# Attention and MLP-mixer kernel: raw buffers of its own for one of the last four weight rows, and v of a unit loaded by one transfer

## The chip, the cores and the metric

The kernel runs on one core of one Trainium2 chip. Five engines work side by side on a core: TensorE (PE, with its weight loads shown apart as PEld), VectorE (DVE), ScalarE (ACT), GpSimd (POOL) and SyncE (SP), which here only issues transfers. The metric is the device time of one execution in microseconds; smaller is better. Several executions are timed, and their median is the kernel's time. One further execution is recorded by the hardware profiler, and all rows shown are from such a record.

## The reference

A linear attention (softmax of q over its features, softmax of k over the sequence) gives a row block x of 576 tokens by 512 features for each of 8 batches, and a mixer follows: one small MLP over the tokens, one over the channels. The weights w come as 64-bit floats, everything else as 32-bit floats.

```python
q_s = softmax(q, axis=-1); k_s = softmax(k, axis=2)        # 8 x 8 heads x 576 x 64
kv = np.einsum('bhsd,bhse->bhde', k_s, v)
x = np.einsum('bhsd,bhde->bhse', q_s, kv)                  # as 8 x 576 x 512
h = np.maximum(xt @ w_tok1, 0.0) @ w_tok2                  # xt: x with tokens last, 576 -> 256 -> 576
u = x + h.transpose(0, 2, 1)
h2 = np.maximum(u @ w_ch1, 0.0) @ w_ch2                    # 512 -> 1536 -> 512
return (u + h2).astype(np.float32)
```

## The kernel before

**Units and groups.** The attention and the token MLP go by units: one batch and two heads, 128 columns, 32 units in all (NU). The channel MLP goes by groups of 512 tokens, nine in all (NG). The first eight units (two batches, NE) are worked off first, in an early stage with buffers of its own; from then on the remaining units are woven into the channel MLP of earlier groups.

**The channel MLP.** w_ch1 and w_ch2 are cut into twelve rows f of 128 hidden features (NF). A step of the list `steps` is one group and one row: `ch1` multiplies the group's u by row f of w_ch1 into a PSUM bank (L482), ACT and DVE turn that into a high part and a low part of h (L485, L486), and one step later `ch2` multiplies h by row f of w_ch2 into four accumulators (L642). The list runs group 0 with rows 0 to 3, group 1 with rows 0 to 11, group 0 with rows 4 to 11 (24 steps up to n0), and then the other groups. From group 3 on the products are made pairwise by a faster scheme (`pair_a`, `pair_b`, L593) out of matrices that were prepared from the rows and written to memory.

**Loading a weight row.** Each weight is a 64-bit number, and the kernel makes 32-bit ones of them itself. `load_weights` brings a piece of 128 x 512 raw numbers (512 KB) into a raw tile by SP (L196). `narrow` does the conversion: DVE takes the exponent out (L232), ACT rescales it (L233), DVE puts in the sign (L234), makes the fraction (L235, L237) and multiplies the two (L239) into a tile cv_s. Then `split` writes a high part by ACT (L130) and a low part by DVE (L131) into the row's place in c1h and c1l, or c2h and c2l. The narrowed piece of w_ch1 is also stored to memory from cv_s by ACT's queue (`whole`, L290). Rows 0 to 7 go two at a time through wide raw tiles (`load_pair`, L222); rows 8 to 11 one at a time (`load_ch`), at steps 7, 8, 10 and 11, each with two pieces: one of w_ch1 and one of w_ch2. Raw tiles come from the pool stg, which has two buffers of 4 KB per partition; cv_s has two buffers too, and `stage_qT` of a unit uses one of them for its transposed q (L393), from which DVE and ACT copy 32-wide blocks (L403) before q's high part qth is cast (L130) for `stage_u` (L459).

**Room.** Pools are stacks on two sides of the on-chip memory. When the early stage ends, its room goes to the tiles of the later units, to c2 of rows 4 to 7, and to the wide raw tiles stg_x and cv_x of rows 4 to 7 (24 KB per partition). When rows 8 to 11 begin, stg_x and cv_x close, and in their place come c2 (16 KB) and c1 (16 KB) of rows 8 to 11. A tile that lies where another lay waits for that one's last reader. After group 2's last steps `stage_pair_pools` closes the c1 pools and puts the pair scheme's tiles there.

**Loading a unit.** `load_unit` brings k transposed (kt), q and k by one transfer each, `load_v` brings v: two transfers of 128 partitions x 4 blocks x 64 (one for each head, L184) and one for the last 64 tokens (L185). In v's tile each block of 64 has a 65th column of ones, so that one matmul (L355) gives both kv and the sum of k; rows 64 to 127 of the last block are zeros, written once by POOL. From unit 8 on there is one v tile, and v of the next unit is asked for when the matmuls on this one are issued.

**What sets the order.** The program is written in one order, and a planner lays out each engine's own order from it when the program is built, with a simulated timeline (`schedule_with_timeline_sim=True`); at run time each engine and each queue goes in that order, so that an instruction whose input is late holds up those behind it. SP's queue takes all loads of weights, q, k and v. `behind(drained)` holds the narrowing of a row, on ACT and DVE, behind the h of the step before.

Of the kernel before, what the change touches and what calls it, by code (L numbers as in the profile page):

```python
# [15 lines left out]
P = 128  # L16
# [4 lines left out]
def attn_mixer_kernel(ctx: ExitStack, tc: tile.TileContext, q, k, kt, v, wt, out, dims):  # L21
# [3 lines left out]
    nc = tc.nc  # L25
    B, H, S, D, TOK, DM, DCH, wide = dims
    NJ = DM // P
    NF = DCH // P
    NT = TOK // P
    C = S // P  # L30
    C1 = C + 1
    S0 = C * P
    TL = S - S0
    NG = B * S // CW
    NU = B * NJ
    NE = 2 * NJ
    F_HEAD, F_MORE = 4, 8
    G_S = 3
    WIDE1, WIDE2 = False, False
    EP = (2, 4)  # L40
# [7 lines left out]
    stg = ctx.enter_context(tc.tile_pool(name="stg", bufs=2))  # L48
    cv = ctx.enter_context(tc.tile_pool(name="cv", bufs=2))
# [10 lines left out]
    def v_tile(pool):  # L60
        t = pool.tile([P, C1, 2, D + 1], F32, name="v_t")
        nc.gpsimd.memset(t[:, :, :, D : D + 1], 1.0)
        nc.gpsimd.memset(t[TL:P, C, :, :], 0.0)
        return t

    v_ring = [v_tile(const)]

    ones = const.tile([P, P], F32, name="ones")
# [24 lines left out]
    c1, c1_pools = {}, {}  # L93

    def c1_rows(f0, f1, side):
        c1_pools[f0] = ExitStack()
        pool = c1_pools[f0].enter_context(tc.tile_pool(name=f"c1_{f0}", bufs=1, side=side))
        t = [pool.tile([P, f1 - f0, NJ, P], F32R, name=f"c1{x}{f0}") for x in "hl"]
        for f in range(f0, f1):
            c1[f] = t, f - f0  # L100
# [8 lines left out]
    def c2_rows(f0, f1):  # L109
        late = ctx.enter_context(tc.tile_pool(name=f"late{f0}", bufs=1))  # L110
        h_ = late.tile([P, f1 - f0, DM], F32R, name=f"c2h{f0}")
        l_ = late.tile([P, f1 - f0, DM], F32R, name=f"c2l{f0}")
        for f in range(f0, f1):
            c2[f] = (h_, l_), f - f0
# [30 lines left out]
    conv = [(stg, cv)]  # L145
    first = []

    @contextmanager
    def behind(instructions):
        with ExitStack() as stack:  # L150
            for ins in instructions:
                stack.enter_context(tc.issue_after(ins))
            yield
# [26 lines left out]
    def load_v(n):  # L180
        if n < NU and n not in v_of:
            t = v_ring[n % 2 if n < NE else 0]
            for h in range(2):
                nc.sync.dma_start(t[:, 0:C, h, 0:D], v[n][:, 0:C, h * D : (h + 1) * D])  # L184
            nc.sync.dma_start(t[0:TL, C, :, 0:D], v[n][0:TL, C, :].rearrange("p (h d) -> p h d", h=2))  # L185
            v_of[n] = t

    def load_weights(i, n=CW, out=None):
# [285 lines left out]
    def ch1(g, f):  # L474
        hh, hl = (h2[:, x, f % 2, :] for x in range(2))
        t = ps_h.tile([P, 512], F32, name="ps_h")
        wh, wl = c1_row(f)
        i = 0
        for n in range(NJ):
            uh, ul = (x[:, n, :] for x in uT[g])  # L480
            for a, w in ((wh, uh), (wl, uh), (wh, ul)):
                nc.tensor.matmul(t, a[:, n, :], w, start=(i == 0), stop=(i == 3 * NJ - 1))  # L482
                i += 1
        drained[:] = [
            nc.scalar.activation(hh, t, AF.Relu).ins,  # L485
            nc.vector.scalar_tensor_tensor(hl, t, 0.0, f32(hh), op0=ALU.max, op1=ALU.subtract).ins,  # L486
        ]
        return hh, hl
# [33 lines left out]
    ring, T, tf, odd, h_slots = [], [], [], [], []  # L522

    def stage_pair_pools(f0):
        c1_pools[f0].close()
        if f0 == 0:
            pool = ctx.enter_context(tc.tile_pool(name="pairs_a", bufs=1, side="right", reuse_waits="tile"))
            for x in "hl":
                T.append(pool.tile([P, 4, CW], F32R, name=f"t{x}"))
            tf.extend(pool.tile([P, CW], F32, name=f"tf{i}") for i in range(2))  # L530
            ring.extend(pool.tile([P, 4, P], F32R, name=f"ring{i}") for i in range(6))
        else:
            pool = ctx.enter_context(tc.tile_pool(name="pairs_b", bufs=1, reuse_waits="tile"))
            odd.extend(pool.tile([P, 2 * CW], F32, name=f"c{i}") for i in range(2))
            h_slots.extend((h2[:, 0, i], h2[:, 1, i]) for i in range(2))
            h_slots.append(tuple(pool.tile([P, CW], F32R, name=f"h3{x}") for x in "hl"))
            ring.extend(pool.tile([P, 4, P], F32R, name=f"ring{i}") for i in range(6, 8))
# [11 lines left out]
    rows = {}  # L549
# [49 lines left out]
    def pair_a(g, p):  # L599

        x = ps_h.tile([P, 512], F32, name="ps_h")
        product(g, P1, x, A)
        product(g, P6, x, Bq)
        c = odd[p % 2]
        c11, both, c22 = c[:, 0:HW], c[:, HW : 3 * HW], c[:, 3 * HW :]
        nc.scalar.copy(c11, x[:, A])
        nc.vector.tensor_tensor(c22, x[:, Bq], c11, op=ALU.add)
        y = ps_h.tile([P, 512], F32, name="ps_h")
        product(g, P5, y, A)
        product(g, P7, y, Bq)  # L610
        nc.vector.tensor_tensor(halves(both), halves(y[:, 0:CW]), c22.unsqueeze(1).broadcast_to([P, 2, HW]), op=ALU.add)
        nc.vector.tensor_tensor(c22, y[:, A], both[:, Bq], op=ALU.add)
        held[0] = c, c11, both

    def pair_b(g, p):

        c, c11, both = held.pop(0)
        x = ps_h.tile([P, 512], F32, name="ps_h")
        product(g, P2, x, A)
        nc.vector.tensor_tensor(c11, x[:, A], c11, op=ALU.add)  # L620
        z = ps_h.tile([P, 512], F32, name="ps_h")
        product(g, P3, z, A)
        product(g, P4, z, Bq)
        nc.vector.tensor_tensor(both, z, both, op=ALU.add)  # L624
        out = []
        for r in (slice(0, CW), slice(CW, 2 * CW)):
            hh, hl = h_slots[at_h[0] % 3]
            at_h[0] += 1
            nc.scalar.activation(hh, c[:, r], AF.Relu)  # L629
            nc.vector.scalar_tensor_tensor(hl, c[:, r], 0.0, f32(hh), op0=ALU.max, op1=ALU.subtract)  # L630
            out.append((hh, hl))
        return out

    def ch2(acc, f, first, last, hh, hl, in_turn=False):

        at = []
        wh, wl = c2_row(f)
        for n, o in enumerate(acc):
            cs = slice(n * P, (n + 1) * P)
            for i, (a, w) in enumerate(((wh, hh), (wl, hh), (wh, hl))):  # L640
                with behind(at):
                    m = nc.tensor.matmul(o, a[:, cs], w, start=(first and i == 0), stop=(last and i == 2))  # L642
                if in_turn:
                    at = [m.ins]
# [79 lines left out]
    load_tok1()  # L724
    first = []
    load_v(0)
    begin(1)
    stages[0][0]()
    soft(1)
    stages[0][1]()  # L730
    load_v(1)
    load_tok2()
    conv[:] = [(stg, cv)]
# [19 lines left out]
    c2_rows(F_HEAD, F_MORE)  # L753
    more_pools = ExitStack()
    wide_pools[:] = [more_pools.enter_context(tc.tile_pool(name=n, bufs=2)) for n in ("stg_x", "cv_x")]

    unit_banks[0] = (ph,)

# [32 lines left out]
    for g in range(2, NG):  # L791
# [8 lines left out]
        put(at - 2, lambda g=g: data_sums(g, (0, 1, 2)))  # L800
        put(at - 1, lambda g=g: data_sums(g, (3,)))
    put(n0 + 8, lambda: stage_pair_pools(0))
    put(n0 + 9, lambda: [load_product() for _ in range(6)])
    put(n0 + 11, lambda: stage_pair_pools(F_MORE))
    put(n0 + 11, lambda: [load_product() for _ in range(2)])

    pend = []
    acc_of = {}
    load_at = {1: F_HEAD, 4: F_HEAD + 2, **dict(zip((7, 8, 10, 11), range(F_MORE, NF)))}
    for i, (g, f) in enumerate(steps):  # L810
        if i in load_at:
            if load_at[i] == F_MORE:
                more_pools.close()
                c2_rows(F_MORE, NF)
                c1_rows(F_MORE, NF, None)
            with behind(drained):
                (load_ch if load_at[i] >= F_MORE else load_pair)(load_at[i])
        more = []
        if g < G_S:
            more = [(f, ch1(g, f))]  # L820
        elif f % 2 == 0:
            pair_a(g, f // 2)
        else:
            more = list(zip((f - 1, f), pair_b(g, f // 2)))
        for fn in todo.pop(i, []):
            fn()
        if pend:
            now = pend.pop(0)
            ch2(*now[1:])
            if now[4]:  # L830
                out_end(*now[:2], i != F_HEAD)
        for fn in todo.pop(i + 0.5, []):
            fn()
        last = i + 1 == len(steps) or steps[i + 1][0] != g
        for ff, h in more:
            new = i == 0 or (g < G_S and steps[i - 1][0] != g) or (g >= G_S and ff == 0)
            if new:
                acc = [ps_o.tile([P, CW], F32, name="ps_o") for _ in range(NJ)]
            pend.append((g, acc, ff, new, last and ff == more[-1][0], *h))
# [62 lines left out]
```

## Time and profile before

| | us |
|---|---|
| median of 3 runs | 813.62 |
| lowest, highest | 811.61, 817.54 |
| the profiled execution | 814.48 |
| its span, first to last instruction | 812.6 |

The profiled execution is 0.9 us above the median of the runs; 1.9 us of it lie around the span. The profile's page gives, for the whole span, the busy time of each engine and a row of 40 digits for each (one digit for every 20.3 us, the busy share in tenths), then groups of instructions by line. The timelines give single instructions: start, duration, engine, line, operation, the tile written, the tiles read, and in brackets the idle time ahead of it and what ended it. "SPq" and "ACTq" are the queues that issue transfers.

The first matmuls of step 0 (L482) start at 81 us. Rows 8 to 11 are narrowed and split between 116 and 177 us.

### The profile page before, as it was taken

To read this page: it belongs to the slowest core of one execution; us is meant where nothing else is said; L and a number is where in the kernel's file an instruction comes from. 1 tells how busy PE (TensorE), PEld (TensorE's weight loads), DVE (VectorE), ACT (ScalarE), POOL (GpSimd) and SP (SyncE) were. 2 spreads that over 40 slices of the span, in tenths; PEclk is the share of its full clock that TensorE was granted. 3 is DMA by queue.
4 is the path that set the end of the run, shared out by engine and by line. 5 is a ranking of instruction groups with operands and counts; after the bars stand their busy time and mean duration, and the time that the engine had idled before them with its cause. 6 is when DMAs were issued, how large, how long until landed. Compare 5 with 4: busy or idle time off the path is not lost.

```text
span 812.6 us, 14046 instructions
## 1 busy us (share of the span) xinstructions
PE 782.8 (96%) x5112; PEld 690.4 (85%) x5112; DVE 605.3 (74%) x1195; ACT 379.9 (47%) x908; POOL 113.8 (14%) x88
## 2 busy tenths in 40 slices
PE   3899999979999999999999999999999999999998
PEld 3688888768878888899999999879999999999996
DVE  7988998789869765987798688877896546436433
ACT  4775533366555654555564455355665522112110
POOL 1000010101212151122212222122122200200000
PEclk9999999999999999999999999999999999999999
DMA  9644632425678643575667656756566445556651
GB/s 300 197 158 146 245 143 92 150 72 188 200 232 283 210 115 98 177 253 175 193 193 243 188 181 186 229 175 191 165 182 209 145 143 179 191 177 205 209 169 52
DMA packets 110852, 147.07 MB, mean 181 GB/s; under 512 B 45760, under 2 KB 57664, under 8 KB 110784
## 3 DMA queue, kind: packets, MB, share of 16 engines
q1 hardware_dynamic: 104448, 134.12, 53.3%
q10 hardware_dynamic: 6336, 12.06, 4.1%
q8 instruction: 41, 0.67, 0.3%
q14 instruction: 27, 0.22, 0.1%
HBM read 122.55 MB, written 23.59 MB: 180 GB/s over the span
## 4 chain that ended last, share of the span: by engine, by line
PE 75%; DVE 11%; DMA 7%; ACT 4%; issue 2%; SPq 1%; POOL 0%; DVEq 0%; ACTq 0%; POOLq 0%
PE ps_o L642 31%; PE ps_h L593 20%; PE ps_h L482 8%; PE ps_h L459 6%; PE ps_h L417 4%; DMA q_t<-in_q 4%; PE ps_h L355 2%; DMA stg<-in_w 1%; ACT q_t L403 1%; PE ps_h L425 1%; DVE q_t L325 1%; DVE q_t L338 1%; PE ps_h L314 1%; DMA k_t<-in_k 1%; DVE st L324 1%
## 5 line engine op out<-in xcount | busy, mean ns | idle before, releaser
L642 PE MATMUL ps_o<-h,c2h 128*128 128x512 f32 x672 | 226.0, 398 | 3.7 <-ACT h L485 3.4
L642 PEld LDWEIGHTS ps_o<-h,c2h 128*128 128x128 f32 x672 | 125.9, 189 | 29.3 <-ACT h L485 4.3
L642 PE MATMUL ps_o<-h,c2l 128*128 128x512 f32 x336 | 132.3, 395 | 0.0
L593 PE MATMUL ps_h<-th,ring 128*128 128x256 f32 x576 | 107.1, 283 | 1.3 <-DVE c L624 1.3
L593 PEld LDWEIGHTS ps_h<-th,ring 128*128 128x128 f32 x576 | 89.7, 191 | 1.5 <-DVE c L624 1.5
L593 PE MATMUL ps_h<-uh,ring 128*128 128x256 f32 x432 | 81.9, 283 | 0.5 <-ACT dg L315 0.5
L593 PE MATMUL ps_h<-tl,ring 128*128 128x256 f32 x288 | 81.4, 283 | 0.0
L593 PEld LDWEIGHTS ps_h<-uh,ring 128*128 128x128 f32 x432 | 70.3, 190 | 5.1 <-ACT dg L315 0.9
L403 ACT COPY q_t<-cv_s 32x160 f32<-32x160 f32 (+1 forms) x232 | 71.9, 310 | 2.8
L316 POOL TENSOR_TENSOR k_t<-k_t,dg 128x640 f32<-128x640 f32 x24 | 40.9, 1704 | 230.5 <-ACT dg L315 215.9
L642 PEld LDWEIGHTS ps_o<-h,c2l 128*128 128x128 f32 x336 | 63.9, 190 | 10.5
L131 POOL TENSOR_TENSOR ql<-q_t,qh 128x640 fp32r<-128x640 f32 x24 | 40.4, 1683 | 182.3 <-ACT qh L130 126.0
L593 PE MATMUL ps_h<-ul,ring 128*128 128x256 f32 x216 | 61.0, 282 | 0.0
L629 ACT ACTIVATE h<-c 128x512 fp32r<-128x512 f32 x48 | 28.9, 625 | 60.2 <-DVE c L624 60.1
L482 PE MATMUL ps_h<-uh,c1h 128*128 128x512 f32 x144 | 56.0, 391 | 0.4 <-ACT c1h L130 0.4
L482 PE MATMUL ps_h<-uh,c1l 128*128 128x512 f32 x144 | 56.2, 390 | 0.0
L482 PE MATMUL ps_h<-ul,c1h 128*128 128x512 f32 x144 | 56.1, 390 | 0.0
L593 PEld LDWEIGHTS ps_h<-tl,ring 128*128 128x128 f32 x288 | 55.2, 192 | 0.0
L466 ACT CAST uh<-ps_h 128x320 fp32r<-128x320 f32 (+4 forms) x76 | 24.8, 336 | 55.7 <-PE ps_h L459 36.5
L334 ACT ACTIVATE q_t<-q_t 128x640 f32<-128x640 f32 x32 | 23.7, 740 | 50.2 <-DVE q_t L325 34.8
L324 DVE TENSOR_REDUCE st<-q_t 128x10 f32<-128x640 f32 x32 | 26.1, 815 | 27.2 <-DMA q_t<-in_q 27.0
L403 DVE COPY q_t<-cv_s 32x160 f32<-32x160 f32 (+1 forms) x152 | 36.7, 241 | 6.8 <-POOL ql L131 5.0
(196 smaller groups left out, 1762.3 us busy)
## 6 DMA issues: line engine op xcount, KB each, us to landing
ring<-w SPq DMA_DIRECT2D x252, 256.0 KB, 3.3
kt_t<-in_kt SPq DMA_DIRECT2D x32, 320.0 KB, 3.3
q_t<-in_q SPq DMA_DIRECT2D x32, 320.0 KB, 3.4
stg_w<-in_w SPq DMA_DIRECT2D x18, 512.0 KB, 6.3
v_t<-in_v SPq DMA_DIRECT2D x64, 128.0 KB, 3.4
k_t<-in_k SPq DMA_DIRECT2D x24, 320.0 KB, 3.8
w<-stg SPq DMA_DIRECT2D x12, 512.0 KB, 3.6
stg<-in_w SPq DMA_DIRECT2D x10, 512.0 KB, 4.8
```

The lines of the kernel that those rows point to most:

```text
L131: lo_eng.tensor_tensor(lo, src, f32(hi), op=ALU.subtract)
L316: nc.gpsimd.tensor_tensor(kx, kx, dg.unsqueeze(1).broadcast_to([P, C1, P]), op=ALU.subtract)
L324: nc.vector.tensor_reduce(st[:, 0, :], qt, axis=AX.X, op=ALU.max)
L334: nc.scalar.activation(qc, qc, AF.Exp)
L403: eng(qx[ys, 0:n, xs], turned[xs, 0:n, ys])
L417: nc.tensor.matmul(y[:, 0:TOK], a, w, start=(i == 0), stop=(i == len(mm) - 1))
L459: nc.tensor.matmul(t[:, 0:N], a, w, start=(i == 0), stop=(i == len(mm) - 1))
L466: nc.scalar.copy(uh, src).ins,
L482: nc.tensor.matmul(t, a[:, n, :], w, start=(i == 0), stop=(i == 3 * NJ - 1))
L593: nc.tensor.matmul(t[:, cols], a, b[:, n], start=(i == 0), stop=(i == 5))
L629: nc.scalar.activation(hh, c[:, r], AF.Relu)
L642: m = nc.tensor.matmul(o, a[:, cs], w, start=(first and i == 0), stop=(last and i == 2))
```

## The change

Three edits, all in the order of the program and in where tiles lie; the arithmetic stays the same.

Row 9 (F_MORE + 1) gets a pool of its own for its raw pieces, `stg_y`, with two buffers of 4 KB per partition. It is opened behind the wide pools when the early stage has ended, and closed at row 10. The c1 tiles of rows 8 to 11 are cut in two: rows 8 and 9 where four rows lay, rows 10 and 11 in a pool opened at row 10, in the room that stg_y leaves. Rows 8, 10 and 11 go on using stg.

v of a unit comes by one transfer of 128 partitions x 10 blocks x 64. The array in memory carries zeros in the last 64 partitions of the last blocks, so that POOL clears there the 65th column alone.

```diff
-    F_HEAD, F_MORE = 4, 8
+    F_HEAD, F_MORE, F_LAST = 4, 8, 10
...
         nc.gpsimd.memset(t[:, :, :, D : D + 1], 1.0)
-        nc.gpsimd.memset(t[TL:P, C, :, :], 0.0)
+        nc.gpsimd.memset(t[TL:P, C, :, D : D + 1], 0.0)
...
-            for h in range(2):
-                nc.sync.dma_start(t[:, 0:C, h, 0:D], v[n][:, 0:C, h * D : (h + 1) * D])
-            nc.sync.dma_start(t[0:TL, C, :, 0:D], v[n][0:TL, C, :].rearrange("p (h d) -> p h d", h=2))
+            nc.sync.dma_start(t.rearrange("p c h d -> p (c h) d")[:, :, 0:D], v[n].rearrange("p c (h d) -> p (c h) d", h=2))
...
     def stage_pair_pools(f0):
+        if f0 == F_MORE:
+            c1_pools[F_LAST].close()
         c1_pools[f0].close()
...
+    next_pools = ExitStack()
+    next_raw = next_pools.enter_context(tc.tile_pool(name="stg_y", bufs=2, side="right"))
...
                 c2_rows(F_MORE, NF)
-                c1_rows(F_MORE, NF, None)
+                c1_rows(F_MORE, F_LAST, None)
+            conv[:] = [(next_raw if load_at[i] == F_MORE + 1 else stg, cv)]
+            if load_at[i] == F_LAST:
+                next_pools.close()
+                c1_rows(F_LAST, NF, None)
...
-    def rows(x):
+    def rows(x, again=None):
         x = x.reshape(nu, 2, s, d)[:, :, twice].reshape(nu, 2, c + 1, P, d)
+        if again is not None:
+            x[:, :, c, tl:] = again
...
-        "in_v": rows(inputs["v"]),
+        "in_v": rows(inputs["v"], 0.0),
```

## The prediction

> **What bounds the kernel now.** I read the page first, for which engine is full and in which of its 40 slices it is not; then TensorE's list of waits, for what those gaps wait on; then the timelines of TensorE (PE), VectorE (DVE), ScalarE (ACT) and SyncE's DMA queue (SP) around the one gap that lies in the change's place.
>
> ```profile
> span 812.6 us, 14046 instructions
> PE 782.8 (96%) x5112; PEld 690.4 (85%) x5112; DVE 605.3 (74%) x1195; ACT 379.9 (47%) x908; POOL 113.8 (14%) x88
> PE   3899999979999999999999999999999999999998
> ```
>
> ```profile
> PE ps_o L304 <- ACT kt_t L301: 5.5, 1, 5.5
> PE ps_o L381 <- issue: 5.4, 1, 5.4
> PE ps_o L642 <- ACT h L485: 3.4, 2, 3.3
> PE ps_h L459 <- ACT qth L130: 1.5, 1, 1.5
> ```
>
> PE is busy for 782.8 of 812.6 us, so 29.8 us are all that waits can ever give back. The two longest waits lie in the first slice, before any weight row of w_ch1 is touched. The slice with a 7 (the ninth, 162 to 183 us) holds the next two, 3.3 us for h and 1.5 us for qth. That is the stage in which the last four weight rows (8 to 11) are loaded, narrowed from 64 bits and split; everything after it keeps PE at 9 tenths. So the change is worth what it does to this one stage.
>
> ```profile
> 157.45 0.51 PE L482 MATMUL ps_h<-uh,c1h 128*128 128x512 f32 x1 [0.45 <-ACT c1h L130]
> 165.81 0.79 PE L642 MATMUL ps_o<-h,c2h 128*128 128x512 f32 x1 [3.28 <-ACT h L485]
> 169.14 0.40 PE L482 MATMUL ps_h<-uh,c1h 128*128 128x512 f32 x1
> 176.52 0.42 PE L459 MATMUL ps_h<-qth,kvh 128*128 128x320 f32 x1 [1.47 <-ACT qth L130]
> ```
>
> ```profile
> 119.57 2.72 PE ps_o L642 x12
> ```
>
> ```profile
> 162.50:165.80 3.30, 0.03 (x1) 0.00 (x0) 2.50 (x6) 3.02 (x7) 0.00 (x0) 0.94 0.58 165
> 165.80:169.10 3.30, 3.29 (x8) 2.67 (x9) 3.30 (x7) 0.62 (x1) 0.00 (x0) 0.54 0.51 142
> ```
>
> The last two rows are windows; the third number from the end is the granted clock. After the stall of 3.28 us the clock is 0.54 for 3.3 us: eight matmuls take 169.14 - 165.81 = 3.33 us, where twelve took 2.72 at full clock (the row of the chain of waits; 0.227 each, 1.82 for eight). So that stall cost 3.28 + 1.51 us. The stall of 1.47 us cost no clock. In all the stage loses 0.45 + 3.28 + 1.51 + 1.47 = 6.7 us.
>
> Now why h is late. In the rows below come SP's issues, one row of the chain of waits, then DVE, then ACT.
>
> ```profile
> 125.17 0.93 SPq L196 DMA_DIRECT2D stg<-in_w  x2
> 146.28 1.66 SPq L196 DMA_DIRECT2D stg<-in_w  x2
> 156.77 2.13 SPq L196 DMA_DIRECT2D stg<-in_w  x2
> 158.99 0.95 SPq L184 DMA_DIRECT2D v_t<-in_v  x2
> ```
>
> ```profile
> 158.57 5.35 DMA stg<-in_w
> ```
>
> ```profile
> 136.08 1.23 DVE L131 TENSOR_TENSOR c2l<-cv_w,c2h 128x1024 fp32r<-128x1024 f32 x1 [1.12 <-ACT c2h L130]
> 139.72 0.42 DVE L232 TENSOR_SCALAR cv_s<-stg 128x512 uint32<-128x512 uint32 x1
> 140.05 0.69 DVE L131 TENSOR_TENSOR c1l<-cv_s,c1h 128x512 fp32r<-128x512 f32 x1
> 150.90 0.43 DVE L232 TENSOR_SCALAR cv_s<-stg 128x512 uint32<-128x512 uint32 x1 [0.86 <-DMA whole<-cv_s]
> 153.11 0.43 DVE L232 TENSOR_SCALAR cv_s<-stg 128x512 uint32<-128x512 uint32 x1 [1.79 <-DMA stg<-in_w]
> 153.46 0.68 DVE L234 SCALAR_TENSOR_TENSOR cv_s<-stg,cv_s 128x512 uint32<-128x512 uint32 x1
> 157.86 0.68 DVE L239 TENSOR_TENSOR cv_s<-stg,cv_s 128x512 f32<-128x512 f32 x1
> 163.95 0.43 DVE L232 TENSOR_SCALAR cv_s<-stg 128x512 uint32<-128x512 uint32 x1 [0.77 <-DMA stg<-in_w]
> 170.49 0.85 DVE L393 STREAM_TRANSPOSE cv_s<-q_t 128x640 f32<-128x640 f32 x1 [0.85 <-DMA whole<-cv_s]
> ```
>
> ```profile
> 151.41 0.73 ACT L233 ACTIVATE cv_s<-cv_s,ebias 128x512 uint32<-128x512 uint32 x1 [3.18 <-DVE cv_s L232]
> 165.16 0.60 ACT L485 ACTIVATE h<-ps_h 128x512 fp32r<-128x512 f32 x1
> 171.23 0.73 ACT L130 CAST qh<-q_t 128x640 fp32r<-128x640 f32 x1 [3.68 <-PE ps_h L417]
> 175.80 0.67 ACT L130 CAST qth<-q_t 128x576 fp32r<-128x576 f32 x1
> ```
>
> Each row's two raw pieces go through the two buffers of stg, so a row's loads are issued only when the row ahead of it has been narrowed: row 9 at 125.17, row 10 at 146.28, row 11 at 156.77. Row 9 doesn't suffer (first read at 139.72, 14 us later). Row 10 does: DVE stands 1.79 us at 153.11. Row 11 does: its second piece is issued at 158.57, lands 5.35 us later, and ACT's step on it (L233) stands in ACT's queue ahead of the h that PE wants.
>
> **The change part by part.** *Row 9 into two buffers of its own.* The four loads of rows 8 and 9 need no turn-taking. Row 9's narrowing doesn't come sooner: it was not waiting for data, and the two cv_s tiles come free with row 8's splits, the last at 140.05. What moves is row 10: it inherits row 9's place, and its loads can be issued at 125.17 in place of 146.28. Row 11 still loads behind row 10's narrowing, in the same two buffers.
>
> Step 1, DVE. Row 10's first L232 stays at 150.90 (it waited for the store out of cv_s). Its second no longer waits 1.79 us, but the L234 behind it needs ACT's L233, which ends at 151.41 + 0.73 = 152.14. L234 thus goes from 153.46 to 152.2: 1.26 us are gained, not 1.79. Step 2, SP. Row 10's last L239 goes from 157.86 to 156.6, and row 11's second load from 158.57 to 157.3. Step 3, landing. With its own 5.35 us it lands 1.26 earlier; with the fastest of this line's loads (3.9 us, next row) 2.7 earlier:
>
> ```profile
> DMA to landing us min/median/max: 3.9/5.3/7.2
> ```
>
> I take 1.5, near its own, since the v and k loads that share the engines with it stand close behind in either case. Step 4, h. L485 goes from 165.16 to 163.65 and PE's restart from 165.81 to 164.3. PE itself arrives 0.45 sooner, as row 10's c1h is no longer late. The stall is then 3.28 - 1.5 + 0.45 = 2.2 us. Step 5, the clock. 2.2 lies between the stall that cost no clock (1.47) and the one that did (3.28), nearer the first: I take no loss, which gains 1.51, and PE is 1.5 + 1.5 = 3.0 us ahead at 169.14.
>
> Step 6 takes a third of that back. PE's next wait is L459 for qth, and qth doesn't follow PE: it follows L393, which waits for the store of row 11's cv_s, a store that follows L232 at 163.95 through the rest of the narrowing. L393 comes 1.5 sooner (169.0), and qth stands 175.80 - 170.49 = 5.31 us behind it, so it comes 1.5 sooner at the least. ACT's part of those 5.31 us begins at 171.23 behind a wait for PE (L417), which comes 3.0 sooner, so ACT may go as much as L393's end allows; between 1.5 and 2.5 I take 2.0. So L459 starts at 174.5, and the wait ahead of it grows from 1.47 to about 2.5 us: the stall has moved rather than gone. This stage gives **2.0 us**, with ends of 1.3 (step 2 alone) and 2.7.
>
> The Trainium skill (TensorE: Matmul & The Clock Gate, Part 1) says that the clock halves after an idle window of about 3.4 us, and that the window runs freely. Here 3.28 us of idling did it, a little under that figure. By that rule neither of the two new stalls would cost any clock and the sum would stay 2.0; by the row here, a stall well under 3.4 can be enough, and with 1.51 us lost once the sum would be 0.5.
>
> *The new buffers' place.* They lie where the early stage was, so row 9's load waits for that stage at most; the wide loads that took the early stage's room were issued at 90.71 (row with the rivals), 49 us ahead of row 9's first reading. Rows 8 and 9 of c1 now take 8 KB per partition where four rows took 16; c1l of row 8 then lies over the wide buffers, whose last reader is the split at 136.08, done at 137.3; it is written at 140.05, behind it. If row 8 were split sooner, that wait would cost at most the 1.2 us of that split. Rows 10 and 11 lie over row 9's raw pieces, whose reading ends ahead of row 10's narrowing (150.90); row 11's first split comes later still. No cost for either.
>
> *v by one transfer.*
>
> ```profile
> L184 SPq DMA_DIRECT2D v_t<-in_v x64: 368/457/1418, 3.5 to 635.1; - x64
> L185 SPq DMA_DIRECT2D v_t<-in_v x32: 601/602/1838, 5.2 to 635.7; - x32
> 42.69 0.33 SPq L161 DMA_DIRECT2D q_t<-in_q  x1
> 184.61 0.80 PE L355 MATMUL ps_h<-v_t,k_t 128*64 128x65 f32 x20
> ```
>
> Three issues of 0.457 + 0.457 + 0.602 = 1.5 us of SP become one. Its price is unknown: not below 0.33 (the issue of a contiguous q_t) and not above the three together; nearest are the 0.46 and 0.60 of the parts, I take 0.6. SP gains 0.9 us per unit, 29 us over 32 units, and the k load behind it starts that much sooner. Nobody on PE waits for it: v issued at 158.99 is first read at 184.61, 25 us later, and no wait of PE's names v or k. The transfer carries 320 KB in place of 288 (zeros for the tail), 1 MB in 147 over the span. The clears on POOL at the start shrink, and nothing waits for them. I cost this part at nothing, from a gain of 0.9 (k sooner once, in a stage where PE waits for it) to a loss of 0.9 (k comes 0.9 sooner into row 11's second load).
>
> **The rivals.**
>
> ```profile
> 90.71 1.76 SPq L222 DMA_DIRECT2D stg_w<-in_w  x4
> stg_w<-in_w SPq DMA_DIRECT2D x4, 512.0 KB, 5.4
> 97.11 0.69 DVE L232 TENSOR_SCALAR cv_w<-stg_w 128x1024 uint32<-128x1024 uint32 x1
> ```
>
> *The whole stage closes.* PE would reach the h at 165.81 - 3.28 - 0.45 = 162.1. If the planner puts h ahead of L233 in ACT's queue and fills PE's wait for qth with matmuls of the next step, all 6.7 us go: 813.6 - 6.7 = 806.9. For it: the order is laid out afresh for the changed program. Against it: without such a change of order L232 would have to start 165.81 - 163.95 = 1.86 us ahead of 162.1, so that the piece lands 2.9 us after its issue at 157.3, and the fastest took 3.9; and L393 hangs on row 11 anyway.
>
> *It doesn't do what it says.* The row that got the buffers was never late (14 us ahead); the late one is row 11, which keeps its turn in stg. If the planner keeps row 10's reading of its pieces where it was, nothing moves: 813.6.
>
> *Slower: row 9's 1 MB goes ahead of rows 4 and 5.* Their four loads of 512 KB were issued at 90.71 to 92.47 and land after 5.4 us in the median, by 97.4, and DVE reads the first at 97.11 without a wait. Four loads in 97.4 - 90.71 = 6.7 us make 3.3 us for two more. If DVE has no slack behind it, rows 8 to 11 and the late h move by that: 813.6 + 3.3 = 816.9. It decides if the new loads stand ahead of L222 in SP's queue by less than 3.3 us; behind it, or well ahead, they cost nothing. Against it: row 9 comes after rows 4 to 7 in the program.
>
> *The clock drops again.* If the stall of 2.2 or of 2.5 us falls so as to halve the clock, 1.5 us go back: 813.1.
>
> **How the numbers follow.** The profiled execution took 814.48 us, 1.9 around a span of 812.6; the median of the runs is 813.62, 0.9 below. 814.48 - 2.0 = 812.5 for such a run, and 813.6 - 2.0 = **811.6** for the median. Chances: the forecast 0.45 (own range 810.9 to 812.3), the whole stage closes 0.13, nothing moves or the clock drops again 0.25, slower by the crowding 0.12, something else in the new order 0.05. All named cases lie from 806.9 to 816.9, so the range is 806.5 to 817.0. Within 1% is 805.5 to 821.8, about what a measurement of this kernel can tell from no change; only the last case and the tails reach beyond: faster 0.06, same 0.89, slower 0.05.
>
> **What would show it.** Right: SP issues row 9's loads before 125 us and row 10's at about 125; DVE has no wait at row 10's second L232; row 11's second load is issued near 157.3; PE's wait for h is 1 to 2.5 us, its wait for qth longer than 1.47; one v issue of about 0.6 us per unit. Wrong: PE's wait for h still 3 us with a granted clock near 0.5 behind it (nothing moved), or neither wait there (all closed), or a DVE wait on stg_w near 97 us (crowding).

## The result, and the profile after

| | before | after |
|---|---|---|
| median, us | 815.30 (10 runs, 811.61 to 817.54) | 809.29 (10 runs, 805.34 to 811.51) |
| the profiled execution, us | 814.48 | 805.34 |
| its span, us | 812.6 | 803.5 |

The ratio of after to before is 0.9927, with a 95% interval of 0.9912 to 0.9942: 6.0 us or 0.7% less, of which the prediction saw 2.0. The profiled execution of after is the fastest of its ten runs; a second recording of the same kernel (below, span 806.0) lies nearer the median, and where sizes matter it is used.

The page of the changed kernel:

```profile
span 803.5 us, 13913 instructions
...
PE 778.6 (97%) x5112; PEld 688.9 (86%) x5112; DVE 606.8 (76%) x1195; ACT 380.2 (47%) x908; POOL 113.1 (14%) x88
...
PE   3899999989999999999999999999999999999998
```

133 instructions fewer than the 14046 before; 64 of them are the issues of v that fell away (two for each of 32 units). The 7 in the ninth slice is gone. TensorE's waits that answer to those shown of before, from its list of waits and from its timeline (start, duration, engine, line, operation, tiles, and in brackets the idle time ahead and what ended it); L483 is the line of h, L457 that of qth's reader:

```profile
PE ps_o L642 <- ACT h L483: 2.4, 2, 1.3
PE ps_h L457 <- ACT qth L130: 1.8, 1, 1.8
```

```profile
161.97 0.50 PE L642 MATMUL ps_o<-h,c2h 128*128 128x512 f32 x1 [1.17 <-ACT h L483]
171.69 0.41 PE L457 MATMUL ps_h<-qth,kvh 128*128 128x320 f32 x1 [1.80 <-ACT qth L130]
189.39 0.50 PE L642 MATMUL ps_o<-h,c2h 128*128 128x512 f32 x1 [1.28 <-ACT h L483]
```

The wait for h went from 3.28 to 1.17 us, and no half-speed clock follows it. The wait for qth grew from 1.47 to 1.80, and a third wait, 1.28 us for a later h, is new. Now the issues of SP and what VectorE does with rows 10 and 11 (L194 is the load of a row, L230 takes the exponent out, L288 on ACT's queue stores the narrowed piece):

```profile
93.42 0.81 SPq L194 DMA_DIRECT2D stg<-in_w  x2
124.34 2.45 SPq L194 DMA_DIRECT2D stg<-in_w  x2
153.30 2.19 SPq L194 DMA_DIRECT2D stg<-in_w  x2
156.99 0.56 SPq L183 DMA_DIRECT2D v_t<-in_v  x1
```

```profile
145.65 0.33 ACTq L288 DMA_DIRECT2D whole<-cv_s  x1
```

```profile
148.60 0.41 DVE L230 TENSOR_SCALAR cv_s<-stg 128x512 uint32<-128x512 uint32 x1
148.93 0.68 DVE L131 TENSOR_TENSOR c2l<-cv_s,c2h 128x512 fp32r<-128x512 f32 x1
149.64 0.43 DVE L230 TENSOR_SCALAR cv_s<-stg 128x512 uint32<-128x512 uint32 x1
157.66 0.43 DVE L230 TENSOR_SCALAR cv_s<-stg 128x512 uint32<-128x512 uint32 x1 [1.14 <-DMA stg<-in_w]
166.49 0.84 DVE L391 STREAM_TRANSPOSE cv_s<-q_t 128x640 f32<-128x640 f32 x1 [0.82 <-DMA whole<-cv_s]
```

Row 9 is issued at 93.42, row 10 at 124.34, row 11 from 153.30 on, where it was 156.77. Neither L230 of row 10 waits. Two things in this listing go beyond the prediction. The first L230 of row 10 starts at 148.60, where it was 150.90, although the store out of its cv_s tile, issued at 145.65, still stands ahead of it: that store landed 2.0 us after its issue, where before it took 4.5 (the experiment with spare loads, below, shows the rows). And the L230 now stands *ahead* of the c2l split of row 9 (L131, 148.93), where before it stood behind: the planner has laid out another order.

How far the gain lies outside the row stage is read from windows (start and end; length, busy time of TensorE, its matmuls, the granted clock, share of the DMA engines, GB/s). Before, and then the second recording of after:

```profile
60.00:110.00 50.00, 49.06 (x284) 1.00 0.47 164
150.00:180.00 30.00, 24.63 (x125) 0.94 0.37 114
500.00:600.00 100.00, 97.84 (x713) 1.00 0.64 192
```

```profile
60.00:110.00 50.00, 50.00 (x286) 1.00 0.56 193
150.00:180.00 30.00, 27.04 (x146) 1.00 0.35 102
500.00:600.00 100.00, 98.98 (x712) 1.00 0.63 192
```

In the stage of rows 10 and 11 (150 to 180) TensorE stands 2.4 us less, and has the full clock (1.51 us in the prediction's rows): about 4 of the 6 us. 0.9 us more come at 60 to 110, where the wait for hl (DVE, at 80 us) is gone, and 1.1 at 500 to 600. Neither of these two places touches a weight row of the change.

### The profile page after: what moved, and what is told of

Read it like the earlier page. It is cut to its first block, busy times and chain, and to the rows that moved or that the text cites. A ratio compares the mean times of both kernels' runs of the same rounds, so it can differ in the third digit from the quotient of the medians.

```text
span 803.5 us, 13913 instructions
## 1 busy us (share of the span) xinstructions
PE 778.6 (97%) x5112; PEld 688.9 (86%) x5112; DVE 606.8 (76%) x1195; ACT 380.2 (47%) x908; POOL 113.1 (14%) x88
## 4 chain that ended last, share of the span: by engine, by line
PE 68%; DVE 13%; issue 9%; DMA 5%; ACT 3%; POOL 2%; SPq 0%; DVEq 0%; POOLq 0%; ACTq 0%
PE ps_o L642 26%; PE ps_h L593 19%; PE ps_h L457 6%; PE ps_h L480 5%; PE ps_h L415 4%; DMA q_t<-in_q 4%; PE ps_h L353 2%; PE ps_o L457 1%; PE ps_h L423 1%; DVE st L322 1%; DVE q_t L323 1%; DVE q_t L401 1%; DVE q_t L336 1%; PE ps_o L415 1%; POOL ql L131 1%
## 5 line engine op out<-in xcount | busy, mean ns | idle before, releaser
L401 ACT COPY q_t<-cv_s 32x160 f32<-32x160 f32 (+1 forms) x232 | 71.8, 310 | 3.2 <-DVE cv_s L391 0.3
L131 POOL TENSOR_TENSOR ql<-q_t,qh 128x640 fp32r<-128x640 f32 x24 | 39.4, 1642 | 178.6 <-DMA kt_t<-in_kt 100.9
L593 PEld LDWEIGHTS ps_h<-ul,ring 128*128 128x128 f32 x216 | 41.0, 190 | 0.1
```

The costliest lines, as they stand in the source:

```text
L131: lo_eng.tensor_tensor(lo, src, f32(hi), op=ALU.subtract)
L401: eng(qx[ys, 0:n, xs], turned[xs, 0:n, ys])
L593: nc.tensor.matmul(t[:, cols], a, b[:, n], start=(i == 0), stop=(i == 5))
```

## The experiments

Each expectation was written before its run. Theories go by letters in them, A to E in the first four; the later ones turn on these: O, the new order carries the gain; S, the time of v's issues and transfers themselves does; D, the store that frees row 10's cv_s lands late when 1 MB of loads is under way beside it; E, a wait seen in the first run with spare loads came from its order; W, the waits that are left are set by what stands ahead in ScalarE's and VectorE's queues. The first question was which of the two parts brings the 6 us.

**The buffers alone.** v keeps its three transfers.

```diff
...
-            nc.sync.dma_start(t.rearrange("p c h d -> p (c h) d")[:, :, 0:D], ...)
+            for h in range(2):
+                nc.sync.dma_start(t[:, 0:C, h, 0:D], v[n][:, 0:C, h * D : (h + 1) * D])
+            nc.sync.dma_start(t[0:TL, C, :, 0:D], ...)
...
```

> Only the raw buffers of row 9 and the cut of c1; v comes by three transfers as before. If the gain lies in the stage of the last four rows (theory A: that stage gives some 4 us, the v transfer some 2 us in the stages of the units behind it), this kernel is about 4 us faster than the one before, with PE's waits for h and qth near 1.2 and 1.8 us, and the small waits of PE between 200 and 240 us (about 1.8 us in all before) still there. If the buffers carry all of it (theory B), it is 6 us faster. If the predicted 2.0 us was right for the buffers and v carries the rest (theory C), it is 2 us faster, with row 10's first exponent step on DVE still held by the store out of cv_s.

814.45 us against 815.68, ratio 0.9990 [0.9974, 1.0005]. Almost nothing: less than the 2.0 predicted, and far from A and B; C's 2 us lies at the edge of the interval. Row 11's second load was indeed issued earlier; yet h came later. ScalarE's timeline of this kernel:

```profile
164.58 0.72 ACT L233 ACTIVATE cv_s<-cv_s,ebias 128x512 uint32<-128x512 uint32 x1 [1.76 <-DVE cv_s L232]
165.21 0.72 ACT L317 ACTIVATE k_t<-k_t 128x640 f32<-128x640 f32 x1
165.84 0.39 ACT L312 ACTIVATE dg<-ident,mc 128x128 f32<-128x128 f32 x1
166.25 0.60 ACT L485 ACTIVATE h<-ps_h 128x512 fp32r<-128x512 f32 x1
```

L232 of row 11's second piece no longer waited for its load; but VectorE was late for it itself, and the planner had put two scalings (L317, L312) between L233 and h, which before stood ahead of L233. TensorE's wait for h was 4.32 us, the clock fell to half behind it, and what was won on the load was given back.

**One transfer for v alone.** Row 9 loads through stg as before.

```diff
...
-                c1_rows(F_MORE, F_LAST, None)
-            conv[:] = [(next_raw if load_at[i] == F_MORE + 1 else stg, cv)]
-            if load_at[i] == F_LAST:
-                next_pools.close()
-                c1_rows(F_LAST, NF, None)
+                c1_rows(F_MORE, NF, None)
...
```

> Only v by one transfer; row 9 keeps its turn in stg. Theory A: about 2 us faster than before, the stall of about 3.3 us for h and the half clock behind it still there, the small waits between 200 and 240 us mostly gone. Theory B: no difference. Theory C: 4 us faster.

810.32 us against 815.68, ratio 0.9938 [0.9913, 0.9962]: 5 us from the part that the prediction had costed at nothing, nearest to C's 4. TensorE still waits for h (0.78 and 2.50 us) with a half-speed clock behind, so the late h is not what it mended. What is gone are other waits: those for c1h and qth in the row stage (0.45 and 1.47 us before), and the one for hl at 80 us (0.9). No buffer of a weight row differs here. The order does: taken by operation, tiles and source line, 1057 of VectorE's 1195 instructions stand in the same sequence in this recording and in that of before; with the buffers alone 1171 do. So the order is a suspect of its own.

**The changed kernel a second time**, as the measure of the others.

> The changed kernel as it is, beside the three others on the same chip, for their comparison and for a second trace. If its first trace is typical, PE waits again about 1.2 us for h and 1.8 us for qth, and the median is 6 us under that of the kernel before. If that trace was a favourable one, the early stage or the stage near 530 us shows 1 to 2 us more of waits.

809.34 us, ratio 0.9920 [0.9895, 0.9945], with the same three waits (1.16, 1.80 and 1.34 us).

**The changed kernel with spare loads.** 1 MB is loaded into row 9's buffers at the moment when the kernel before loaded row 10; nothing of the computation changes.

```diff
+            if load_at[i] == F_MORE + 1:
+                for x in (AT_C1, AT_C2):
+                    nc.sync.dma_start(next_raw.tile(...), wt[x + F_LAST].bitcast(U32))
```

> The changed kernel with 1 MB of spare loads added (two pieces of row 10 once more, into row 9's raw buffers once these have been narrowed; nobody reads them), issued where row 10's loads stood before the change, beside the store out of cv_s. If row 10 starts sooner than predicted because that store no longer shares the transfer engines with row 10's loads (theory D), row 10's first exponent step on DVE waits for the store again, by 1.5 to 2 us, and the kernel loses 1.5 to 3 us against the changed one. If the store is not what holds it (theory E: the order of DVE's queue sets the start), DVE has no wait there, and the time stays within 0.7 us of the changed kernel.

811.65 us, ratio 0.9948 [0.9928, 0.9967], and a wait at row 10's first L230 (0.94 us). But its order differed from the changed kernel's in some places, so the run could not say whether the loads or the order did it. It was repeated with the order held (below).

**Order and parts told apart.** An engine's order can be held by edges between neighbouring instructions that carry no semaphore:

```diff
...
+    info = mybir.DependencyInfo(mybir.DependencyClass.NoSync, mybir.DependencyReason.DATA)
+    for engine, order in want.items():
+        seq = [traced[engine][i] for i in order]
+        for before, ins in zip(seq, seq[1:]):
+            tc.add_manual_dep(ins, before.name, info, reason="in_order")
```

Four kernels were built so. First the changed kernel held to its own order, to see what the holding costs:

> The changed kernel with every engine's order tied to its own, as a measure of what the tying itself costs. If it costs nothing: 808.5 to 810.5 us, ratio 0.991 to 0.995. If the tied runs lose by the tying, 811 us or more, and the two earlier tied runs (811.25 and 814.08) must be read with that loss taken off.

810.28 us, ratio 0.9930 [0.9906, 0.9953]: nothing that can be told. (The kernel before was not run with its own order held.) Then the changed kernel's order with the buffers, but three transfers for v; the order of before with one transfer; and the order of before with both parts:

> The two raw buffers for row 9, v of a unit by three transfers as in the kernel before, and the order of every engine's instructions tied to the one that the changed kernel has; the three issues of v stand where the one stood. Theory O (one transfer for v is worth its time because the planner, which charges for every issue, lays out another order): the gain stays, 808.5 to 810.5 us against 815 of the kernel before. Theory S (the time of the issues and of the smaller transfers themselves): as with the buffers alone, 813.5 to 815.5 us.

> v of a unit by one transfer, the raw buffers as before, and the order of every engine's instructions tied to that of the kernel before. Theory O: no gain, 814.5 to 816 us. Theory S: as with one transfer alone, 809.5 to 811 us.

> Both parts of the change, with every engine's order tied to that of the kernel before. Theory O (the order carries most of the gain; buffers and one transfer bring 0.8 and 1.7 us by themselves): 812.5 to 814 us. Theory S (the parts carry it by themselves): 809 to 810.5 us.

| order | row 9's buffers | v | median, us | ratio to before, 95% |
|---|---|---|---|---|
| before's | no | 3 | (815 to 816) | 1 |
| its own, near before's | yes | 3 | 814.45 | 0.9990 [0.9974, 1.0005] |
| before's, held | no | 1 | 814.08 | 0.9985 [0.9968, 1.0003] |
| before's, held | yes | 1 | 812.83 | 0.9963 [0.9947, 0.9980] |
| its own, near the changed one's | no | 1 | 810.32 | 0.9938 [0.9913, 0.9962] |
| the changed one's, held | yes | 3 | 811.25 | 0.9951 [0.9934, 0.9968] |
| the changed one's, its own | yes | 1 | 809.29 | 0.9927 [0.9912, 0.9942] |

Rows that differ in one thing give its worth (difference of ratios by 815 us). The order: 3.2 (buffers, three transfers), 2.9 (buffers, one transfer), 3.8 (no buffers). The one transfer in a given order: 1.2, 2.2 and 2.0. The buffers: 0.8, 1.8 and 0.9. Each single difference is uncertain by some 2 us, but the three of a kind agree: of 6 us about 3 are the order, 1 to 2 the transfer itself, about 1 the buffers, none of whose three differences can be told from nothing by itself. Theory O holds for about half; with three transfers in the changed order 811.25 lies between what O and S expected.

What one transfer does by itself is spread thin. In the order of before TensorE's waits between 180 and 300 us fell from 1.8 to 1.2. In the changed order the recording with three transfers stands 0.4, 0.6 and 0.4 us more than the second one of the changed kernel at 150 to 180, 180 to 300 and 500 to 600 us. It also has one step at half clock (the last section), but that is of this one execution: the mean clock over its nine runs, 0.997, is the same as over the ten of the changed kernel. Why the planner chooses another order when 64 issues fall away was not tried.

**The store beside loads.** The spare loads again, with the order on TensorE, VectorE, ScalarE and GpSimd held to the changed kernel's.

> The changed kernel with 1 MB of spare loads where row 10's loads are issued (nothing of the computation changes), with the order on TensorE, VectorE, ScalarE and GpSimd tied to that of the changed kernel. Theory D (the store of the half row takes longer to land when 1 MB of loads is under way beside it, and the first narrowing of row 10 waits for it): a wait of 1.5 to 2 us at that narrowing, the store landing more than 4 us after its issue, and 810.5 to 812 us. Theory E (the wait came from the other order of the first run with spare loads): no wait there, and within 0.7 us of the changed kernel's 809.3.

810.67 us, ratio 0.9941 [0.9919, 0.9963]. ACT's queue, VectorE and TensorE:

```profile
147.39 0.35 ACTq L288 DMA_DIRECT2D whole<-cv_s  x1
```

```profile
151.95 0.43 DVE L230 TENSOR_SCALAR cv_s<-stg 128x512 uint32<-128x512 uint32 x1 [1.53 <-issue]
```

```profile
165.59 0.50 PE L642 MATMUL ps_o<-h,c2h 128*128 128x512 f32 x1 [3.02 <-ACT h L483]
```

Same order, and yet L230 stands 1.53 us. The profile names no releaser for this wait, but it has the store's own landing. For the one store issued near 146 us, in the changed kernel and then with the spare loads:

```profile
DMA to landing us min/median/max: 2.0/2.0/2.0
```

```profile
DMA to landing us min/median/max: 4.5/4.5/4.5
```

Issued at 147.39, it landed at 151.9, and L230 starts at 151.95. This is D's wait, of D's size, and behind it the wait for h is back at 3.02. All thirteen recordings divide in the same way, whatever their order: the store takes 4.5 us in the five where 1 MB of loads is issued within 2 us of it (before, the one transfer alone and in the order of before, the two with spare loads), and 2.0 in the other eight. So the buffers have an effect that the prediction lacked: by moving row 10's 1 MB away from 146 us they let the store land sooner. What it is worth here is small, some 1 us by the ratios (0.9941 against 0.9930 and 0.9927 without the loads), which lies within the intervals.

**Two attempts to go further.** First, the second piece of row 11 narrowed and split four steps later, behind the first unit's qth:

```diff
+        if f == NF - 1:
+            ... (load only)
+            return
...
+        if i == 15:
+            with behind(drained):
+                finish_ch()
```

> The changed kernel, with the second half of row 11 loaded where it was but narrowed and split four steps later, behind the first unit's qth on ScalarE. Theory W (TensorE's two waits of 1.2 and 1.8 us after the rows are set by ScalarE's work on row 11, which stands ahead of h and qth): both go, and the time is 806 to 807.5 us. Rival: the split of row 11 is late for the hidden step that multiplies by it, one wait of 1 to 3 us takes the place of the two, and the time is 808.5 to 811 us.

814.21 us, ratio 0.9976 [0.9961, 0.9990]: worse than the changed kernel and than either expectation, and W not tested by it, since the planner filled the place with other work. Eight copies for qth (L411) now stood ahead of h; a third wait came up later, for ul:

```profile
160.29 2.56 ACT L411 COPY q_t<-cv_s 32x160 f32<-32x160 f32 x8
162.88 0.74 ACT L325 ACTIVATE k_t<-k_t 128x640 f32<-128x640 f32 x1
163.52 0.39 ACT L320 ACTIVATE dg<-ident,mc 128x128 f32<-128x128 f32 x1
163.81 0.57 ACT L493 ACTIVATE h<-ps_h 128x512 fp32r<-128x512 f32 x1
```

```profile
164.44 0.79 PE L652 MATMUL ps_o<-h,c2h 128*128 128x512 f32 x1 [2.22 <-ACT h L493]
265.35 0.39 PE L425 MATMUL ps_h<-w1h,qh 128*128 128x256 f32 x1 [2.36 <-DVE ul L475]
```

Second, the changed kernel with its order held but for a few moves by hand; nothing else is changed. On ScalarE:

```diff
 L315 k_t
+L483 h of step 14
 L310 dg
 L231 row 11, second piece
-L483 h of step 14
...
-L130 c2h of row 11
 L343 qh
 L130 qth
 L483 h
+L130 c2h of row 11
...
+L483 h (189 us)
 L363 kvf
-L483 h (189 us)
```

On VectorE a maximum for k (L295) goes behind row 11's first L237, and row 11's second L237 and c2l go behind the copies for qth (L401).

> The changed kernel in its own order but for seven instructions moved on ScalarE and VectorE: h of step 14 ahead of row 11's second exponent and a scaling, the last split of row 11 behind the first unit's qth on ScalarE (its multiplication behind the transposing copies on VectorE), and one later h ahead of a scaling that waits for a reciprocal. Theory W (the three waits of 1.2, 1.8 and 1.3 us are set by what stands ahead in these two queues): the first and third shrink to 0.3 or less, the second to about 1.1, and the time is 806.5 to 808 us. Rival: what is moved back is late in its turn, no gain or a loss, 809 us or more.

807.34 us against 815.63, ratio 0.9903 [0.9877, 0.9929], the lowest median of all; the changed kernel held to its own order, timed beside it, had 0.9930, and the two intervals overlap. TensorE's three waits:

```profile
162.92 0.50 PE L642 MATMUL ps_o<-h,c2h 128*128 128x512 f32 x1 [0.35 <-ACT h L483]
172.24 0.42 PE L457 MATMUL ps_h<-qth,kvh 128*128 128x320 f32 x1 [1.20 <-ACT qth L130]
190.16 0.50 PE L642 MATMUL ps_o<-h,c2h 128*128 128x512 f32 x1 [1.42 <-ACT h L483]
```

The first two went nearly as W expected (0.35 and 1.20), the third did not: 1.42 in place of 0.3. Its h was moved ahead of kvf, but still stands behind the issue of a result's store (L671), which is late:

```profile
189.12 0.34 ACTq L671 DMA_DIRECT2D out<-stg  x1
189.51 0.60 ACT L483 ACTIVATE h<-ps_h 128x512 fp32r<-128x512 f32 x1 [0.99 <-DVE st L335]
```

## Why the prediction was right or wrong, step by step

The time, 809.29, lies within the range, but below the forecast's own range of 810.9 to 812.3. That it is only 2.3 us from the 811.6 is in part luck: the three runs of before that the forecast started from had a median of 813.62, the ten have 815.30, and 2.0 less than that is 813.3. The gain was three times the one forecast.

The signs named for "right" all came: loads of row 9 at 93.42 and of row 10 at 124.34, no wait at row 10's second L230, row 11's second load at 155.2, waits of 1.17 for h and 1.80 for qth, 0.56 us for v. They don't show the forecast's mechanism, though: with both parts in the order of before, on which every term of the sum was worked out, h is waited for 2.69 us and the clock falls to half. There the two parts brought 3.0 us (1.6 to 4.3 by the interval); the 2.0 lies within, by other terms.

*Step 1, VectorE.* The second L232 of row 10 lost its wait, as said. That the first "stays at 150.90 (it waited for the store out of cv_s)" is wrong: I took the store's landing as given, but it was late because row 10's own loads ran beside it, as the spare loads show (4.5 against 2.0 us to land). Moving loads moved the store too.

*Steps 2 to 4, row 11 and h.* In the order of before, the very ground of the sum, adding the buffers to one transfer took the wait for h from 3.25 to 2.69 us (rows of the two kernels held to it); 2.2 was said. With the buffers alone it rose to 4.32, since the landing had ceased to be what h waits for, and the order of ScalarE and VectorE decided. The step "L485 goes from 165.16 to 163.65" holds only as long as the load is last; I had not asked what is next behind it on the same two engines.

```profile
166.83 0.80 PE L640 MATMUL ps_o<-h,c2h 128*128 128x512 f32 x1 [3.25 <-ACT h L483]
```

```profile
168.83 0.80 PE L642 MATMUL ps_o<-h,c2h 128*128 128x512 f32 x1 [2.69 <-ACT h L483]
```

*Step 5, the clock.* "2.2 lies between ... I take no loss, which gains 1.51" is wrong. In the order of before 2.69 us cost a step at half clock, and with row 11 late 2.22 did. The 1.51 that I counted came in the changed kernel only because its wait was 1.17. The prediction named this as a rival (chance 0.25 together with "nothing moves") where it should have been the forecast.

*Step 6.* The wait for qth did grow, from 1.47 to 1.80 and not to 2.5, and stayed at 1.48 in the order of before.

*The new buffers' place* cost nothing: TensorE is busy for 50.00 of 50 us at 60 to 110, where the wide loads and row 9's share the queue. The crowding rival did not come up.

*v by one transfer* is the step that failed: "I cost this part at nothing". Its price was right (0.56 us an issue, 0.6 said). That no wait of TensorE names v or k was a loose reading: three rows of its list name kt or k, but put the wait down to ScalarE's work on them, none to a load. But the part was argued with the order of before, as if that order stayed. It did not: the layout changed on every engine, and that brought about 3 us, a part of it where I had not looked. The wait for hl at 80 us (0.9 us in before) stands in the four recordings in the order of before or near it and in none of the other nine. The 1.1 us at 500 to 600 do not go with the order: the wait there is 0.7 to 1.3 us in recordings of the changed order too. The one transfer itself brought 1 to 2 us more, beyond the bound of 0.9 that I gave it, though that excess is no larger than what the intervals leave open.

*The rivals.* "The whole stage closes" had the right mechanism ("the order is laid out afresh for the changed program") and nearly the right size (6.7; 6.0 came), but not the right place: about 4 us came in the stage, which did not close (1.17 and 1.80 us are left), and the rest from elsewhere. I gave it 0.13 and treated the order as a condition of one stage, when it is a property of the whole program.

## What to carry to other kernels

Where a planner lays out the order, cost a change in two parts, the change in the order of before and the new order, and give the second a spread of its own (here about 3 us of 6); holding the orders by edges without semaphores separates the two. When a late load is brought forward, ask what the same instruction waits for next, and which stores and loads shared the engines with it: a store may have been late only because of that load.

## What the runs showed of the hardware

**The clock is granted in steps, and half a step of idling is enough.** In all thirteen recordings the changes of the granted clock lie on a fixed grid of 3.41 us, and amid the work half clock lasts one step. The clock falls in the step behind one in which TensorE stood for about half or more. Two recordings of the same order of instructions have the same wait of 1.9 us near 28 us. In the changed kernel held to its own order it lies within one step:

```profile
27.58:31.00 3.42, 1.50 (x9) 1.00 0.91 274
31.00:34.41 3.41, 3.41 (x23) 0.50 0.41 123
```

In the first recording of the changed kernel the grid cuts it, and nothing happens:

```profile
28.28:31.69 3.41, 1.74 (x13) 1.00 0.86 300
31.69:35.10 3.41, 3.41 (x33) 1.00 0.35 111
```

With the changed order and three transfers, a wait of 1.85 us fell within one step and cost a half-speed step, about 1.7 us; waits of 1.80 in the same place did not:

```profile
169.69:173.11 3.42, 1.57 (x10) 1.00 0.00 0
173.11:176.52 3.41, 3.41 (x10) 0.50 0.05 15
```

From 20 us on and up to the last matmuls of each recording, seventeen steps with 1.67 us of idling or more were followed by half clock, and none with less; between 1.67 and 1.81 both occur. The clock goes with a part of the scatter of a kernel's runs: among the ten of the changed kernel the one with a mean clock of 1.000 took 805.34 us, the three with 0.995 took 809.29 to 810.96. The Trainium skill (TensorE: Matmul & The Clock Gate, Part 1) gives a free-running window of about 3.4 us, with which the grid agrees, and asks for an idle window before the clock halves; here about half a window was enough.

**VectorE beside GpSimd.** An L233 of 128x512 takes 0.42 us; the one that ran beside GpSimd's scaling of k took over four times that, in before (1.79, as L235) and after alike. In the changed kernel an L237 beside GpSimd took 1.74 us at 167.26, where others take 0.68; but a transpose (L391) at 201.96 beside GpSimd took the 0.84 that it takes alone at 170.98, so not every instruction is slowed. Rows of the changed kernel; no run took the neighbour away, so the cause is not shown:

```profile
141.67 0.42 DVE L233 TENSOR_SCALAR stg<-stg 128x512 uint32<-128x512 uint32 x1
143.21 1.80 DVE L233 TENSOR_SCALAR stg<-stg 128x512 uint32<-128x512 uint32 x1
```

```profile
142.87 1.85 POOL L314 TENSOR_TENSOR k_t<-k_t,dg 128x640 f32<-128x640 f32 x1 [37.49 <-ACT dg L313]
```
